# Hyena convolution with two MoE layers on one core: staged rows written in two halves, and an inverse transform in split fp32r from tile 21 on

## The chip, the cores and the metric

The kernel runs on one core of a Trainium2 chip. The metric is the device time of one launch in microseconds (us); of several runs the median is told.

## What is computed

The reference, cut to what matters:

```python
B, S, D = 2, 12480, 128
h_filt = (np.maximum(pos_emb @ w1, 0.0) @ w2) * np.exp(-0.01 * pos)[:, None]
u = x * v
Uf = np.fft.rfft(u, n=2 * S, axis=1)
Hf = np.fft.rfft(h_filt, n=2 * S, axis=0)
y = np.fft.irfft(Uf * Hf[None], n=2 * S, axis=1)[:, :S, :]
x = (x * y).reshape(B * S, D)
h = x @ moe_w_in
x = (h * np.clip(h + 3.0, 0.0, 6.0) / 6.0) @ moe_w_out
h = np.maximum(x @ moe2_w_in, 0.0)
out = h * h @ moe2_w_out
```

A long convolution along the sequence, a gate with x, and two feed-forward layers of 128 x 2048 x 128.

## The kernel before

**Convolution.** The FFT is done by matmuls. Iteration i of the main loop (some 96 of them) handles four channels and one of three signals: the filter or one of the two batches. It runs `s1` (a transform over n1, float32, 180 columns), `twiddle` (DVE, partly POOL), `split1` (ACT makes the high part h, POOL the low part l), `s2` (a transform over n2 in three fp32r matmuls of high and low parts, 360 columns), then `filt` or `prod`, `s3` (float32, back over n2) and `keep`, in which ACT gathers the result in a staging tile `stg`. Sixteen channels make a block; there are eight blocks. The loop is a software pipeline written by hand: in each round `split1` (line 202) stands ahead of `filt` or `prod`, and `keep` (line 257) at the end.

After the last `keep` of a block ACT also issues the block's rows to DRAM: `write(blk, 0)`, two small writes to `zda` (rows of tiles 0 to 3), and `write(blk, 1)`, two writes to `zdb` of 1350 KB each (the other tiles), one for each half of the 128 rows (line 360).

**Tiles.** There are 64 tiles of 390 tokens. Layer 0 of tile j and layer 1 of tile j - 20 alternate: tiles 0 to 20 of layer 0 first, then pairs (0, j), (1, j - 20), at last layer 1 alone. A tile has eight steps q. In each step PE does `l1` (six fp32r matmuls of 390 columns, line 519) and, three steps late, `l2` (six more, line 565); ACT makes `r` (relu) and `gh`, the high part of `g`; DVE makes `g` (line 535 or 538); the low part `gl` (line 548) is made by DVE in even steps and by POOL in odd ones.

Between them stands the way into layer 0. `loads` brings za, zb, the table vt and xt of a tile; `combine` (POOL, line 449) adds and subtracts za and zb to pp and pn; `s4` (line 463) is the inverse transform over k1: for each of four parts u two float32 matmuls (r = 0, 1) of 98 or 97 columns with pp or pn as weights and vt as what moves. `s4` is a generator; `between` sends one matmul at a time into PE's stream, two in a step, in steps 4 to 7 of (0, j) for tile j + 1. `gate` (line 472) multiplies the result by x, `gate_split` makes its high and low parts oh and ol (lines 478, 479), and `part1` those of layer 1, xh and xl (lines 589, 590).

The order on each engine is the order in which the program is written; nothing reorders it.

Of the kernel before, what the change touches and what calls it, by code (L numbers as in the profile page):

```python
# [7 lines left out]
F32 = mybir.dt.float32  # L8
F32R = mybir.dt.float32r
U32 = mybir.dt.uint32  # L10
AF = mybir.ActivationFunctionType
ALU = mybir.AluOpType
# [25 lines left out]

@with_exitstack
def tile_hyena_moe(ctx: ExitStack, tc, xg, vg, xT, pos, w1d, w2d, win, fmat, twc,  # L40
                   tws, dcs, inv, vtab, w_in1, w_out1, w_in2, w_out2, out):
    nc = tc.nc
    PSUM = bass.MemoryType.PSUM

# [17 lines left out]

    hs = [hp.tile([128, 32, 128], F32, tag=f"h{q}", name=f"h{q}") for q in range(4)]

    wsrc = [w_in1, w_out1, w_in2, w_out2]
    wh = {0: cp.tile([128, 2, FF], F32R, name="wp0")}

# [63 lines left out]


    def tile_loads(j, za, zb, v, x):
        nc.sync.dma_start(v, vtab[j])
        nc.sync.dma_start(x, xT[j])
        nb = NBLK - (j == 0)
        for h, t in enumerate((za, zb)):
            zr = zds[0][h, j] if j < ZA else zds[1][h, j - ZA]
            nc.sync.dma_start(t.rearrange("k d r b c -> k d (r b c)")[:, :nb],
                              zr[:nb].rearrange("d k c -> k d c"))  # L140
# [110 lines left out]
    def keep(i):  # L251
        g, s = divmod(i, 3)
        blk, ch0 = g // 4, (g % 4) * 4
        ps = ps3s.pop(i)
        if blk not in stg:
            stg[blk] = sp.tile([128, K1, 2, 2, 16], F32, name=f"stg{blk}", tag="stg")
        nc.scalar.activation(
            stg[blk][:, :, :, s - 1, ch0:ch0 + 4].rearrange("p k r c -> p r c k"),
            ps[:, :, :K4].rearrange("p r (c k) -> p r c k", c=4), AF.Copy)
        if g % 4 == 3 and s == 2:  # L260
            sv = stg.pop(blk).rearrange("p k r b c -> p k (r b c)")
            if blk == NBLK - 1:

                for h, t in enumerate((za, zb)):
                    nc.scalar.dma_start(t.rearrange("k d r b c -> k d (r b c)")[:, blk], sv[64 * h:64 * h + 1])
                tail.append(sv)
            write(blk, 0, sv)
            if blk < NBLK - 1:
                write(blk, 1, sv)


    with tc.tile_pool(name="mlp", bufs=2, side="right") as mp, \
# [83 lines left out]
    with tc.tile_pool(name="cv_ps", bufs=4, space=PSUM) as vps:  # L356
        def write(blk, z, sv, queue=nc.scalar):
            lo, hi = ((0, ZA), (ZA, 64))[z]
            for h in range(2):
                queue.dma_start(zds[z][h, :, blk], sv[64 * h + lo:64 * h + hi])  # L360

        tail = []
        s1(0)
        twiddle(0)
        s2(1)
        s1(3)
        split1(0)
        twiddle(3)
        s2(2)
        product(1, 0)  # L370
        product(1, 1)
        load(2, 0)
        load(2, 1)
        for i in range(NI + 2):

            a, z = i + AH, i - 2
            if i < NI and i not in (1, 2):
                s2(i)
            if 3 < a < NI:
                s1(a)  # L380
            if 0 <= z < NI and z % 3:
                s3(z)
            if 2 < a - 1 < NI:
                split1(a - 1)
            if 0 <= i < NI:
                if i % 3 == 0:
                    filt(i)
                else:
                    prod(i)
            if 3 < a < NI:  # L390
                twiddle(a)
            if 0 <= z < NI and z % 3:
                keep(z)
            if i == 27:
                raw_weight(1)

            for t, f in ((a + 6, load), (a + 3, product)):
                g, s = divmod(t, 3)
                if s and (2 if f is load else 1) < g < G:
                    f(g, s - 1)  # L400
            if i == NI - 1:

                room = hp.tile([128, 2, 3, FF // 4], F32, tag="h2", name="room")
                room0 = hp.tile([128, 7, 512], F32, tag="h3", name="room0")
                other = parts[(1, 3)] = decoding(None, 1, 3, nc.gpsimd)
                for _ in range(5):
                    next(other)
                decode(None, 1, 0)
                next(other)
                next(other)  # L410
                parts[(1, 1)] = decoding(None, 1, 1)
                for _ in range(5):
                    next(parts[(1, 1)])
                za, zb = (room0[:K1, k].rearrange("k (d r b c) -> k d r b c", d=NBLK, r=2, b=2) for k in (0, 1))
                vt = {0: room0[:K1, 2, :4 * N1].rearrange("k (q r n) -> k q r n", q=2, r=2)}
                xt = {0: room0[:, 3, :TOK]}
                tile_loads(0, za, zb, vt[0], xt[0])
# [7 lines left out]
    def loads(j):  # L425
        za = mo.tile([K1, NBLK, 2, 2, 16], F32, name=f"za{j}", tag="za")
        zb = mo.tile([K1, NBLK, 2, 2, 16], F32, name=f"zb{j}", tag="zb")
        vt[j] = mo.tile([K1, 2, 2, N1], F32, name=f"vt{j}", tag="vt")
        xt[j] = mo.tile([128, TOK], F32, name=f"xt{j}", tag="xt")
        tile_loads(j, za, zb, vt[j], xt[j])  # L430
        zt[j] = (za, zb)

    def combine(j):
# [13 lines left out]
        for k in range(2):  # L447
# [2 lines left out]
                                        (ALU.add, ALU.subtract)[k])  # L450
            yield

    py, ob = {}, {}

    def s4(j):

        ps = mps.tile([128, 512], F32, name=f"py{j}", tag="acc", bufs=2)
        v = vt.pop(j)
        for u in range(4):
            q, b = divmod(u, 2)  # L460
            o, n = UOFF[u]
            for r in range(2):
                nc.tensor.matmul(ps[:, o:o + n], pm[j][q][:, r, b, :],  # L463
                                 v[:, q, r, :n], start=(r == 0), stop=(r == 1))
                if u == 3 and r == 1:
                    pm.pop(j)
                    py[j] = ps
                yield

    def gate(j):  # L470
        ob[j] = mo.tile([128, TOK], F32, name=f"o{j}", tag="o")
        nc.vector.tensor_tensor(ob[j], py.pop(j)[:, :TOK], xt.pop(j), ALU.mult)

    def gate_split(j):
        o = ob.pop(j)
# [3 lines left out]
        nc.vector.tensor_tensor(l, o, h.bitcast(F32), ALU.subtract)  # L479
        xin[(0, j)] = (h, l)  # L480

    AHEAD = 20
    order = []
    for j in range(NT + AHEAD):
        if j < NT:
# [86 lines left out]
    def finish(l, j):  # L572
        ps = acc.pop((l, j))[:, :TOK]
        if l == 0:

            x1[j] = mr.tile([128, TOK], F32, name=f"x1{j}", tag="x1", bufs=AHEAD + 1)
            nc.scalar.activation(x1[j], ps, AF.Copy, scale=1.0 / 6.0)
        else:
            ot = mr.tile([128, TOK], F32, name=f"ot{j}", tag="ot")
            nc.scalar.activation(ot, ps, AF.Copy)  # L580
            nc.scalar.dma_start(out[j], ot)

# [41 lines left out]
    for n in range(len(steps) + LAG + 1):  # L624
        if n < len(steps):
            l, j, q = steps[n]
            l1(n)
        m = n - LAG
        if 0 <= m < len(steps):
            l2(m)  # L630
        if 0 <= m - 1 < len(steps) and steps[m - 1][2] == NP - 1:
            finish(*steps[m - 1][:2])
        if n < len(steps):
            if l == 0 and j < AHEAD and QS < q < QS + 3:
                (gate if q == QS + 1 else gate_split)(j + 1)
            if l == 1 and j + AHEAD + 1 < NT and q < 2:
                (gate_split if q else gate)(j + AHEAD + 1)
            if q == 6 and n + 2 < len(steps) and steps[n + 2][0] == 1:
                part1(steps[n + 2][1])
            relu(n)  # L640
            act(n)
        if 0 <= n - 1 < len(steps):
            split(n - 1)
        if n < len(steps):


            t, at = (j, (4, 7)) if l == 0 else (j + AHEAD, (1, 3))
            if t < AHEAD or l == 1:
                if q == at[0] and t + 2 < NT:
                    sums = combine(t + 2)  # L650
                if q in at and t + 2 < NT:
                    next(sums)
                if q == at[0] + 2 and t + 3 < NT:
                    loads(t + 3)

            for _ in range(2 if n < 14 else int(q not in (QS + 1, QS + 2))):
                next(rest, None)


def _tables():  # L660
# [17 lines left out]
    tt = 128 * n1[None, None, None, :] + pair[:, None, :, None]  # L678
    ph = 2 * np.pi * ((tt * (2 * k1[None, :, None, None] + 1)) % (2 * n)) / (2 * n)
    vtab = np.stack([np.cos(ph), -np.sin(ph)], axis=3) * (2.0 / n)  # L680
    pos = np.arange(S, dtype=np.float32)
    win = np.zeros(SP, np.float32)
    win[:S] = np.exp(np.float32(-0.01) * pos)
    assert not win[LF - S:].any()
    f = lambda z: np.ascontiguousarray(z, dtype=np.float32)
    return dict(win=f(np.repeat(win.reshape(N1, 2, 64).transpose(1, 2, 0).reshape(2, 64 * N1), 64, axis=0)), fmat=f(fmat), twc=f(twc), tws=f(tws),
                dcs=f(dcs), inv=f(inv), vtab=f(vtab))


def _token_index():  # L690
# [58 lines left out]
```

## Time and profile before

| | us |
|---|---|
| median of 3 runs (2830.41 to 2832.78) | 2831.36 |
| the profiled execution | 2832.95 |
| its span in the profile | 2831.1 |
| PE busy | 2765.9 (98%) |
| DVE busy | 2112.1 (75%) |
| ACT busy | 2021.9 (71%) |
| POOL busy | 1569.1 (55%) |

The span runs from the first to the last instruction; 1.85 us of the execution lie around it. PE is TensorE's matmuls, PEld its weight loads, DVE VectorE, ACT ScalarE, POOL GpSimd, SP the engine that issues most loads. A q behind an engine's name is its sequencer. PE's busy time overstates its work, since matmuls overlap and their ends are modelled. A row of a timeline gives a start, a duration, what ran how often, and in brackets the idle time before it and what ended that. Names stand as out<-in, with line numbers of the kernel before.

### The profile page before, as it was taken

How to read it: one execution, taken by the hardware profiler on the slowest of the kernel's cores; microseconds unless marked ns; L12 is line 12 of the kernel's file. 1: busy time of each engine (PE TensorE's matmuls, PEld its weight loads, DVE VectorE, ACT ScalarE, POOL GpSimd, SP SyncE). 2: the span in 40 equal slices, each digit the busy share in tenths (PEclk: the TensorE clock that was granted, in tenths of full speed). 3: DMA queues.
4: the chain of work that ended last, by engine and by line, in shares of the span. 5: the costliest groups of instructions: out<-in, count | busy, mean ns of one | idle time of the engine just before them, and what ended most of it. 6: DMA issues, size and time to landing. Idle time of an engine off the chain costs nothing.

```text
span 2831.1 us, 42236 instructions
## 1 busy us (share of the span) xinstructions
PE 2765.9 (98%) x15712; PEld 2712.0 (96%) x15712; DVE 2112.1 (75%) x2270; ACT 2021.9 (71%) x2694; POOL 1569.1 (55%) x1030
## 2 busy tenths in 40 slices
PE   7999998899999999999999999999999999999999
PEld 5888887799999999999999999999999999999999
DVE  6888888897987777777777777777777777666666
ACT  6444445687777777777777777777777777777777
POOL 3888786566665544555455545545545545444444
PEclk9999999899999999999999999999999999999999
DMA  5243433412111110001111111011111110000000
GB/s 160 92 148 105 135 110 87 108 39 71 38 35 41 27 25 23 25 25 27 27 27 27 27 27 27 24 27 27 27 27 27 27 27 17 7 12 12 12 12 15
DMA packets 139420, 125.79 MB, mean 44 GB/s; under 512 B 99692, under 2 KB 122702, under 8 KB 137806
## 3 DMA queue, kind: packets, MB, share of 16 engines
q1 hardware_dynamic: 128322, 89.23, 11.6%
q10 hardware_dynamic: 10892, 33.86, 4.0%
q8 instruction: 124, 2.03, 0.3%
q14 instruction: 82, 0.67, 0.1%
HBM read 86.64 MB, written 36.37 MB: 43 GB/s over the span
## 4 chain that ended last, share of the span: by engine, by line
PE 88%; DVE 4%; issue 3%; POOL 2%; ACT 2%; DMA 1%; ACTq 0%; POOLq 0%; SPq 0%; DVEq 0%
PE acc L565 38%; PE ph L519 38%; PE p L217 4%; PE py L463 4%; PE p L178 2%; PE p L248 1%; DVE a L194 1%; POOL l L203 1%; DVE b L188 1%; DVE p L192 1%; POOL a L241 0%; ACT h L331 0%; POOL v L155 0%; POOL a L194 0%; DVE b L236 0%
## 5 line engine op out<-in xcount | busy, mean ns | idle before, releaser
L548 POOL TENSOR_TENSOR gl<-g,gh 128x780 fp32r<-128x780 f32 x532 | 1006.1, 1891 | 1114.3 <-ACT gh L545 1109.4
L565 PE MATMUL acc<-gh,wp 128*128 128x390 f32 x4096 | 921.5, 346 | 8.0 <-DVE wp L119 8.0
L545 ACT ACTIVATE gh<-g 128x780 fp32r<-128x780 f32 x1024 | 866.6, 846 | 15.1 <-DVE g L535 13.1
L535 DVE SCALAR_TENSOR_TENSOR g<-r,ph 128x780 f32<-128x780 f32 x512 | 493.9, 965 | 338.5 <-POOL gl L548 295.0
L565 PEld LDWEIGHTS acc<-gh,wp 128*128 128x128 f32 x4096 | 730.2, 189 | 8.3 <-issue 8.3
L538 DVE SCALAR_TENSOR_TENSOR g<-ph,r 128x780 f32<-128x780 f32 x512 | 496.2, 969 | 265.1 <-POOL gl L548 240.0
L526 ACT ACTIVATE r<-ph,three 128x780 f32<-128x780 f32 x512 | 467.8, 914 | 279.5 <-PE ph L519 268.8
L519 PE MATMUL ph<-oh,wp 128*128 128x390 f32 x2048 | 633.5, 349 | 1.3 <-ACT oh L478 1.3
L519 PE MATMUL ph<-xh,wp 128*128 128x390 f32 x2048 | 616.9, 342 | 0.0
L528 ACT ACTIVATE r<-ph 128x780 f32<-128x780 f32 x512 | 422.2, 825 | 255.0 <-PE ph L519 252.6
L565 PE MATMUL acc<-gl,wp 128*128 128x390 f32 x2048 | 533.6, 341 | 3.4 <-POOL gl L548 1.7
L548 DVE TENSOR_TENSOR gl<-g,gh 128x780 fp32r<-128x780 f32 x492 | 516.1, 1049 | 0.0
L519 PEld LDWEIGHTS ph<-oh,wp 128*128 128x128 f32 x2048 | 383.8, 190 | 1.5 <-ACT oh L478 1.5
L565 PEld LDWEIGHTS acc<-gl,wp 128*128 128x128 f32 x2048 | 377.1, 189 | 5.0 <-DVE gl L548 2.6
L519 PEld LDWEIGHTS ph<-xh,wp 128*128 128x128 f32 x2048 | 380.7, 189 | 0.0
L519 PE MATMUL ph<-ol,wp 128*128 128x390 f32 x1024 | 349.4, 341 | 1.6 <-DVE ol L479 1.6
L519 PE MATMUL ph<-xl,wp 128*128 128x390 f32 x1024 | 347.6, 339 | 0.0
L202 ACT ACTIVATE h<-a 128x720 fp32r<-128x720 f32 x96 | 76.6, 804 | 221.4 <-DVE a L194 133.7
L203 POOL TENSOR_TENSOR l<-a,h 128x720 fp32r<-128x720 f32 x96 | 168.1, 1751 | 93.8 <-ACT h L202 93.8
L519 PEld LDWEIGHTS ph<-ol,wp 128*128 128x128 f32 x1024 | 193.9, 189 | 2.3 <-DVE ol L479 2.3
L519 PEld LDWEIGHTS ph<-xl,wp 128*128 128x128 f32 x1024 | 193.0, 188 | 0.0
L479 DVE TENSOR_TENSOR ol<-o,oh 128x390 fp32r<-128x390 f32 x64 | 118.4, 1850 | 10.2 <-ACT oh L478 10.2
(91 smaller groups left out, 2702.7 us busy)
## 6 DMA issues: line engine op xcount, KB each, us to landing
zdb<-stg ACTq DMA_DIRECT2D x14, 1350.0 KB
x<-xg SPq DMA_DIRECT2D x64, 196.0 KB
v<-vg SPq DMA_DIRECT2D x64, 196.0 KB
out<-ot ACTq DMA_DIRECT2D x64, 195.0 KB
xt<-xT SPq DMA_DIRECT2D x63, 195.0 KB
za<-zdb SPq DMA_DIRECT2D x60, 180.0 KB
zb<-zdb SPq DMA_DIRECT2D x60, 180.0 KB
vt<-vtab SPq DMA_DIRECT2D x63, 137.8 KB
```

The source lines that it names most:

```text
L203: nc.gpsimd.tensor_tensor(l, gt, h.bitcast(F32), ALU.subtract)
L217: nc.tensor.matmul(pv, wt, x, start=(n == 0), stop=(n == len(ops) - 1))
L463: nc.tensor.matmul(ps[:, o:o + n], pm[j][q][:, r, b, :], v[:, q, r, :n], start=(r == 0), stop=(r == 1))
L479: nc.vector.tensor_tensor(l, o, h.bitcast(F32), ALU.subtract)
L519: nc.tensor.matmul(ps[:, c, :TOK], wt, x, start=(m == 0), stop=(m == 2))
L526: nc.scalar.activation(r, ph[n][:, :, :TOK], AF.Relu, bias=three)
L528: nc.scalar.activation(r, ph[n][:, :, :TOK], AF.Relu)
L535: nc.vector.scalar_tensor_tensor(g, r, 6.0, pv, ALU.min, ALU.mult)
L538: nc.vector.scalar_tensor_tensor(g, pv, 0.0, r, ALU.max, ALU.mult)
L545: nc.scalar.activation(h, g, AF.Copy)
L548: eng.tensor_tensor(l, g, h.bitcast(F32), ALU.subtract)
L565: nc.tensor.matmul(ps, wt, x, start=(q == 0 and m == 0), stop=(q == NP - 1 and m == len(ops) - 1))
```

## The change

It has two parts. The first: `write(blk, 1)` no longer stands behind the last `keep` of a block. Its two writes go to a list, and each round of the convolution's loop that has no `keep` issues one of them on ACT.

The second: for tiles above 20, `halve` makes a high and a low part of pp and pn (ACT and DVE), POOL casts the table of the tile, which now comes from the host as a high and a low half (`vsplit`), and `s4` does three fp32r matmuls (low x high, high x low, high x high) for each float32 one, three to a yield. The output of a part is always 98 columns wide, so `gate` takes two instructions, one for each pair of parts. `halve` is called in steps 4 and 6 of (1, j), two tiles ahead, and for tile 21 in steps 0 and 1 of (0, 20). Buffers of `o` and `ot` go from two to one, those of `x1` from 21 to 20.

```diff
             write(blk, 0, sv)
             if blk < NBLK - 1:
-                write(blk, 1, sv)
+                late_rows.extend((blk, h, sv) for h in range(2))
...
             if 0 <= z < NI and z % 3:
                 keep(z)
+            elif late_rows:
+                blk, h, sv = late_rows.pop(0)
+                nc.scalar.dma_start(zds[1][h, :, blk], sv[64 * h + ZA:64 * h + 64])
...
-        nc.sync.dma_start(v, vtab[j])
+        nc.sync.dma_start(v, vtab[j] if j <= AHEAD else vsplit[j])
...
+    def halve(j, k):
+        t = pm[j][k]
+        h = mo.tile([K1, 2, 2, D], F32R, name=f"ph{j}_{k}", tag=f"pph{k}", bufs=1)
+        l = mo.tile([K1, 2, 2, D], F32R, name=f"pl{j}_{k}", tag=f"ppl{k}", bufs=1)
+        nc.scalar.activation(h, t, AF.Copy)
+        nc.vector.tensor_tensor(l, t, h.bitcast(F32), ALU.subtract)
+        if not k:
+            vr[j] = mo.tile([K1, 2, 2, 2, N1], F32R, name=f"vr{j}", tag="vr", bufs=1)
+            nc.gpsimd.tensor_copy(vr[j], vt.pop(j))
+        halves.setdefault(j, []).append((h, l))
+        if k:
+            pm[j] = halves.pop(j)
...
+        if j > AHEAD:
+            v = vr.pop(j)
+            for u in range(4):
+                q, b = divmod(u, 2)
+                hi, lo = pm[j][q]
+                ops = [(p[:, r, b, :], v[:, k, q, r, :]) for p, k in ((lo, 0), (hi, 1), (hi, 0))
+                       for r in range(2)]
+                for m, (wt, x) in enumerate(ops):
+                    nc.tensor.matmul(ps[:, N1 * u:N1 * u + N1], wt, x, start=(m == 0), stop=(m == 5))
+                    if m % 3 == 2:
+                        if u == 3 and m == 5:
+                            pm.pop(j)
+                            py[j] = ps
+                        yield
+            return
...
-        ob[j] = mo.tile([128, TOK], F32, name=f"o{j}", tag="o")
-        nc.vector.tensor_tensor(ob[j], py.pop(j)[:, :TOK], xt.pop(j), ALU.mult)
+        ob[j] = mo.tile([128, TOK], F32, name=f"o{j}", tag="o", bufs=1)
+        ps, x = py.pop(j), xt.pop(j)
+        if j <= AHEAD:
+            nc.vector.tensor_tensor(ob[j], ps[:, :TOK], x, ALU.mult)
+            return
+        for c, n in ((0, 98), (196, 97)):
+            o, xx = (t[:, c:c + 2 * n].rearrange("p (b n) -> p b n", b=2) for t in (ob[j], x))
+            pv = ps[:, c:c + 2 * N1].rearrange("p (b n) -> p b n", b=2)
+            nc.vector.tensor_tensor(o, pv[:, :, :n], xx, ALU.mult)
...
-            x1[j] = mr.tile([128, TOK], F32, name=f"x1{j}", tag="x1", bufs=AHEAD + 1)
+            x1[j] = mr.tile([128, TOK], F32, name=f"x1{j}", tag="x1", bufs=AHEAD)
...
-            ot = mr.tile([128, TOK], F32, name=f"ot{j}", tag="ot")
+            ot = mr.tile([128, TOK], F32, name=f"ot{j}", tag="ot", bufs=1)
...
                 if q == at[0] + 2 and t + 3 < NT:
                     loads(t + 3)
+                if l == 1 and q in (4, 6) and t + 2 < NT:
+                    halve(t + 2, q // 6)
+            elif j == AHEAD and q < 2:
+                halve(j + 1, q)
```

Three places in the order of instructions. The first is ACT at the end of a block of the convolution, before (stg is the staging tile, h the high part that split1 makes, hr and hq what filt makes):

```order
L257 ACTIVATE stg_819<-p_11_1181 128x2x4x90
L360 DMA zda<-stg_819 4x5760 x2
L360 DMA zdb<-stg_819 60x5760 x2
L202 ACTIVATE h_16_1226<-a_16_1193 128x720
L202 ACTIVATE h_17_1266<-a_17_1235 128x720
```

and with the change:

```order
L258 ACTIVATE stg_819<-p_11_1181 128x2x4x90
L362 DMA zda<-stg_819 4x5760 x2
L203 ACTIVATE h_16_1224<-a_16_1193 128x720
L398 DMA zdb<-stg_819 60x5760
L203 ACTIVATE h_17_1265<-a_17_1233 128x720
```

The first zdb write moves behind the next split, h_16; the second stands behind h_19, three rounds later.

The second place is PE in step 4 of a tile of layer 0, before (py is what s4 writes, ph what l1 writes, acc what l2 writes):

```order
L519 MATMUL ph_16112<-oh_15869,wp_79 128x390
L463 MATMUL py_16119<-vt_15558,pp_15881 128x98
L565 MATMUL acc_40_16094<-gh_16083,wp_4292 128x390 x4
L565 MATMUL acc_40_16094<-gl_16084,wp_4292 128x390 x2
L463 MATMUL py_16119<-vt_15558,pp_15881 128x98
L519 MATMUL ph_16136<-oh_15869,wp_79 128x390
```

and with the change:

```order
L564 MATMUL ph_11423<-oh_11170,wp_79 128x390
L490 MATMUL py_11430<-vr_11266,pl_0_11263 128x98 x2
L490 MATMUL py_11430<-vr_11266,ph_0_11262 128x98
L610 MATMUL acc_27_11405<-gh_11394,wp_4292 128x390 x4
L610 MATMUL acc_27_11405<-gl_11395,wp_4292 128x390 x2
L490 MATMUL py_11430<-vr_11266,ph_0_11262 128x98 x3
L564 MATMUL ph_11451<-oh_11170,wp_79 128x390
```

Where one float32 matmul stood, three of fp32r stand; the matmuls around them keep their places.

The third is DVE in steps 4 to 7 of a tile of layer 1, before:

```order
L538 SCALAR_TENSOR_TENSOR g_9939<-ph_9924,r_9937 128x780
L538 SCALAR_TENSOR_TENSOR g_9960<-ph_9945,r_9958 128x780
L548 TENSOR_TENSOR gl_9963<-g_9939,gh_9962 128x780
L538 SCALAR_TENSOR_TENSOR g_9981<-ph_9966,r_9979 128x780
L538 SCALAR_TENSOR_TENSOR g_10002<-ph_9987,r_10000 128x780
```

and with the change (pl is the low part of pp or pn):

```order
L583 SCALAR_TENSOR_TENSOR g_11256<-ph_11241,r_11254 128x780
L467 TENSOR_TENSOR pl_0_11263<-pp_11182,ph_0_11262 90x512
L583 SCALAR_TENSOR_TENSOR g_11283<-ph_11268,r_11281 128x780
L593 TENSOR_TENSOR gl_11286<-g_11256,gh_11285 128x780
L583 SCALAR_TENSOR_TENSOR g_11304<-ph_11289,r_11302 128x780
L467 TENSOR_TENSOR pl_1_11311<-pn_11183,ph_1_11310 90x512
L583 SCALAR_TENSOR_TENSOR g_11329<-ph_11314,r_11327 128x780
```

One subtraction stands behind the g of step 4, and one behind that of step 6.

## Rows read from the trace of the kernel before

**Rows 1.** The page: the chain that ended last, by engine.
```profile
PE 88%; DVE 4%; issue 3%; POOL 2%; ACT 2%; DMA 1%; ACTq 0%; POOLq 0%; SPq 0%; DVEq 0%
```

**Rows 2.** Windows: the stretch, its length, busy us (instructions) of each engine, clock, DMA.
```profile
core 0: us, PE busy (x) PEld busy (x) DVE busy (x) ACT busy (x) POOL busy (x), PEclk, DMA share, GB/s
75.00:490.00 415.00, 392.29 (x2112) 352.70 (x2110) 348.42 (x411) 199.17 (x259) 334.21 (x218) 0.98 0.38 114
...
905.00:2430.00 1525.00, 1525.00 (x8791) 1525.00 (x8790) 1099.25 (x1142) 1159.36 (x1520) 766.12 (x506) 1.00 0.10 26
```

**Rows 3.** Timeline of ACT and its queue around the end of a block.
```profile
176.40 0.81 ACT L202 ACTIVATE h<-a 128x720 fp32r<-128x720 f32 x1 [4.56 <-DVE a L194]
...
181.18 1.51 ACT L257 ACTIVATE stg<-p 128x720 f32<-128x720 f32 x1
182.72 0.59 ACTq L360 DMA_DIRECT2D zda<-stg  x2
183.35 5.88 ACTq L360 DMA_DIRECT2D zdb<-stg  x2
189.28 1.50 ACT L202 ACTIVATE h<-a 128x720 fp32r<-128x720 f32 x2 [6.59 <-DMA zda<-stg]
```

**Rows 4.** Timeline of PE at the same place.
```profile
190.14 0.60 PE L217 MATMUL p<-h,dcl 128*128 128x360 f32 x2 [1.29 <-DVE a L192]
191.93 0.60 PE L217 MATMUL p<-l,dch 128*128 128x360 f32 x2 [1.18 <-POOL l L203]
```

**Rows 5.** Windows of 20 us: the slice with that place, and the next.
```profile
180.00:200.00 20.00, 17.53 (x86) 15.55 (x85) 14.25 (x17) 8.89 (x11) 14.04 (x10) 0.91 0.70 206
200.00:220.00 20.00, 20.00 (x114) 18.37 (x113) 17.89 (x21) 8.99 (x14) 16.99 (x12) 1.00 0.52 159
```

**Rows 6.** The page: DMA issues of the big staged writes on ACT's queue.
```profile
zdb<-stg ACTq DMA_DIRECT2D x14, 1350.0 KB
```

**Rows 7.** Windows: the first and the last of four stretches behind a block.
```profile
138.25:141.65 3.40, 2.86 (x9) 2.86 (x10) 0.00 (x0) 1.79 (x3) 3.40 (x4) 0.50 0.97 341
...
455.70:459.10 3.40, 3.40 (x13) 3.40 (x13) 1.62 (x2) 0.34 (x2) 3.33 (x3) 0.50 0.88 307
```

**Rows 8.** Timeline of PE: starts of l2 in a plain step, then with py.
```profile
1512.15 0.88 PE L565 MATMUL acc<-gh,wp 128*128 128x390 f32 x4
...
1514.30 0.88 PE L565 MATMUL acc<-gh,wp 128*128 128x390 f32 x4
...
1516.59 0.96 PE L565 MATMUL acc<-gh,wp 128*128 128x390 f32 x4
...
1519.19 0.97 PE L565 MATMUL acc<-gh,wp 128*128 128x390 f32 x4
```

**Rows 9.** Timeline of PE's weight loads behind one transform.
```profile
1517.57 0.37 PEld L463 LDWEIGHTS py<-vt,pp 90*128 90x128 f32 x2
1517.86 0.19 PEld L519 LDWEIGHTS ph<-oh,wp 128*128 128x128 f32 x1
1517.97 0.19 PEld L519 LDWEIGHTS ph<-ol,wp 128*128 128x128 f32 x1
1518.15 0.37 PEld L519 LDWEIGHTS ph<-oh,wp 128*128 128x128 f32 x2
```

**Rows 10.** Groups: count, busy us, mean ns, idle before; 905 to 2430 us, then all.
```profile
L548 POOL TENSOR_TENSOR gl<-g,gh 128x780 fp32r<-128x780 f32 x338 | 635.5, 1880 | 759.3 <-ACT gh L545 759.3
...
L115 ACT ACTIVATE wp<-wa 128x512 fp32r<-128x512 f32 x12 | 7.5, 621 | 0.0
```

**Rows 11.** Groups of DVE from 905 to 2430 us: two subtractions of one shape.
```profile
L479 DVE TENSOR_TENSOR ol<-o,oh 128x390 fp32r<-128x390 f32 x42 | 81.3, 1936 | 7.9 <-ACT oh L478 7.9
...
L590 DVE TENSOR_TENSOR xl<-x,xh 128x390 fp32r<-128x390 f32 x43 | 24.0, 558 | 0.0
```

**Rows 12.** Timelines of DVE and of PE in a tile of layer 1.
```profile
1467.00 0.97 DVE L538 SCALAR_TENSOR_TENSOR g<-ph,r 128x780 f32<-128x780 f32 x1 [0.91 <-POOL gl L548]
1467.89 0.96 DVE L548 TENSOR_TENSOR gl<-g,gh 128x780 fp32r<-128x780 f32 x1
...
1470.30 0.52 PE L565 MATMUL acc<-gl,wp 128*128 128x390 f32 x2
```

**Rows 13.** Timeline of DVE soon after the convolution.
```profile
519.76 4.83 DVE L117 TENSOR_TENSOR room<-room,wp 128x512 f32<-128x512 f32 x1
```

More of the change, by code (lines that the diff above doesn't have):

```diff
@@ L40, in tile_hyena_moe @@
 def tile_hyena_moe(ctx: ExitStack, tc, xg, vg, xT, pos, w1d, w2d, win, fmat, twc,
-                   tws, dcs, inv, vtab, w_in1, w_out1, w_in2, w_out2, out):
+                   tws, dcs, inv, vtab, vsplit, w_in1, w_out1, w_in2, w_out2, out):
     nc = tc.nc
@@ L63, in tile_hyena_moe @@
     hs = [hp.tile([128, 32, 128], F32, tag=f"h{q}", name=f"h{q}") for q in range(4)]
+    AHEAD = 20
     wsrc = [w_in1, w_out1, w_in2, w_out2]
@@ L360, in write @@
                 queue.dma_start(zds[z][h, :, blk], sv[64 * h + lo:64 * h + hi])
-        tail = []
+        tail, late_rows = [], []
         s1(0)
@@ L427, in loads @@
         zb = mo.tile([K1, NBLK, 2, 2, 16], F32, name=f"zb{j}", tag="zb")
-        vt[j] = mo.tile([K1, 2, 2, N1], F32, name=f"vt{j}", tag="vt")
+        if j <= AHEAD:
+            vt[j] = mo.tile([K1, 2, 2, N1], F32, name=f"vt{j}", tag="vt")
+        else:
+            vt[j] = mo.tile([K1, 2, 2, 2, N1], F32, name=f"vt{j}", tag="vt")
         xt[j] = mo.tile([128, TOK], F32, name=f"xt{j}", tag="xt")
@@ L451, in combine @@
             yield
+    def halve(j, k):
[10 more added lines that the diff above has]
+            pm[j] = halves.pop(j)
+    halves, vr = {}, {}
     py, ob = {}, {}
@@ L457, in s4 @@
         ps = mps.tile([128, 512], F32, name=f"py{j}", tag="acc", bufs=2)
-        v = vt.pop(j)
+        v = vt.pop(j, None)
+        if j > AHEAD:
[13 more added lines that the diff above has]
+            return
         for u in range(4):
@@ L470, in gate @@
     def gate(j):
-        ob[j] = mo.tile([128, TOK], F32, name=f"o{j}", tag="o")
-        nc.vector.tensor_tensor(ob[j], py.pop(j)[:, :TOK], xt.pop(j), ALU.mult)
+        ob[j] = mo.tile([128, TOK], F32, name=f"o{j}", tag="o", bufs=1)
+        ps, x = py.pop(j), xt.pop(j)
+        if j <= AHEAD:
+            nc.vector.tensor_tensor(ob[j], ps[:, :TOK], x, ALU.mult)
[4 more added lines that the diff above has]
+            nc.vector.tensor_tensor(o, pv[:, :, :n], xx, ALU.mult)
     def gate_split(j):
@@ L480, in gate_split @@
         xin[(0, j)] = (h, l)
-    AHEAD = 20
     order = []
@@ L680, in _tables, with top @@
     vtab = np.stack([np.cos(ph), -np.sin(ph)], axis=3) * (2.0 / n)
+    def top(z):
+        m, e = np.frexp(z)
+        return np.ldexp(np.round(m * 4096), e - 12)
+    vt = np.stack([np.cos(ph), -np.sin(ph)], axis=3) * (2.0 / n)
+    vhi = top(vt)
     pos = np.arange(S, dtype=np.float32)
@@ L686, in _tables @@
     return dict(win=f(np.repeat(win.reshape(N1, 2, 64).transpose(1, 2, 0).reshape(2, 64 * N1), 64, axis=0)), fmat=f(fmat), twc=f(twc), tws=f(tws),
-                dcs=f(dcs), inv=f(inv), vtab=f(vtab))
+                dcs=f(dcs), inv=f(inv), vtab=f(vtab),
+                vsplit=f(np.stack([vhi, top(vt - vhi)], axis=2)))
 def _token_index():
@@ L736 @@
     names = ["xg", "vg", "xT", "pos", "w1d", "w2d", "win", "fmat", "twc", "tws", "dcs",
-             "inv", "vtab", "w_in1", "w_out1", "w_in2", "w_out2"]
+             "inv", "vtab", "vsplit", "w_in1", "w_out1", "w_in2", "w_out2"]
     aps = [nc.dram_tensor(n, arrays[n].shape, mybir.dt.from_np(arrays[n].dtype),
```

## The prediction

> **What bounds the kernel now.** I read the chain of work that ended last first: 88% of the span is PE [rows 1], so a microsecond of PE work is a microsecond of time unless PE stands still for another reason. Then the stages: in the convolution (75 to 490 us) PE is busy 392 of 415 us; from 905 to 2430 us, where tiles 21 to 63 go through the inverse transform, it is busy without a gap, at full clock, while DVE, ACT and POOL have 28%, 24% and 50% to spare [rows 2]. The change touches both stages, so each is costed by itself: in the second PE work counts in full, in the first what counts is why PE stands still. The profile's column of idle time per line comes last, for the engines beside PE.
>
> **Why PE stands still in the convolution.** After the last keep of each block of 16 channels ACT issues four staged writes in a row; the two big ones hold it for 5.88 us, and its next split waits 6.59 us for them [rows 3]. PE runs dry behind that split, twice, 1.29 and 1.18 us, 2.47 together [rows 4]; the slice from 180 to 200 us misses just that much, its neighbour none [rows 5]. Fourteen big writes stand on ACT's queue [rows 6], so seven blocks pay. After four of the seven stalls the granted clock falls from 1.00 to 0.50 (from 2.4 to 1.2 GHz) for some 3.4 us, from 138 us the first time and from 456 us the last [rows 7].
>
> **Part 1, staged rows in two halves.** The two big writes of a block leave their place behind the keep and go out one by one, in the iterations without a keep, three iterations apart, behind that iteration's split. No byte more is written, and SP's queue keeps its order. Each half holds ACT for about 2.9 us (half of 5.88). Behind the split of that iteration ACT stands idle 4.56 us now, waiting for DVE [rows 3], so the issue fits with some 1.6 us over, and the small writes that stay behind the keep (0.59 us) are no longer than the work that PE has queued. I take the stalls as gone: 7 x 2.47 = 17.3 us. With the stalls gone the clock has no cause to fall: half of PE's busy time in those stretches, 1.4 us in the first and 1.7 in the last [rows 7], some 6.5 us in four. Sum **-23.8 us**. Ends: -27 if the records hide a little of each stall behind a matmul's modelled end, -6 if each half still holds the split up for half of the stall and only the clock is won back.
>
> **Part 2, the matmuls.** A plain step of twelve 390-column matmuls takes 2.15 us from one acc to the next (1512.15 to 1514.30); a step with two float32 transforms takes 2.60 (1516.59 to 1519.19) [rows 8]. So one float32 matmul of 98 columns costs 0.225 us. It shows as two records with a weight load each (py x2), hence 0.1125 a record. Is that the columns or the loads? Twelve matmuls of 390 columns in 2.15 us are 0.46 ns a column, so 98 columns are 0.045 us; and right behind a transform the loads follow one another at 0.11 us (1517.86, 1517.97), of fp32r weights too [rows 9], where between 390-column matmuls they are 0.18 apart. A short matmul is paced by its weight load. The change makes six fp32r matmuls of two float32 ones, each with other weights than the one before, so three loads stand in place of two: 3 x 0.1125 = 0.3375 us. By tile eight such groups, 2.70 us in place of 1.80, and 43 tiles (21 to 63): 43 x 8 x 0.1125 = **+38.7 us**, on PE, which waits for nobody there. Ends from the rows: if columns alone counted, 3 x 0.045 = 0.135 us a group, -31 us; if each fp32r matmul of 98 columns were as dear as a float32 one of the same size, 0.675 a group, +155 us. I stay by the loads, since rows 9 have exactly that case, fp32r loads behind short matmuls.
>
> A rule of the Trainium skill speaks against me: FP8 and Floating Point Precision, section TensorE Precision Notes, counts a true fp32 matmul as four passes through the array. Three single passes for four would be a quarter off, 0.25 x 0.225 x 344 = -19 us, an estimate by that page. The trace's 0.225 us is five times the 0.045 of one pass of 98 columns, so passes are not what is paid here.
>
> **Part 3, the splitting.** For each tile from 21 on ACT rounds 2 x 512 elements (0.62 us each by the 512-element copy), DVE subtracts twice, POOL casts the table (784 elements; no cast by POOL is in the trace, so between nothing and the 1.88 us of its two-input subtraction of 780) [rows 10]. All three have room [rows 2] in a pair of tiles, which is 16 x 2.15 + 8 x 0.225 = 36.2 us long; what matters is the moment. The DVE subtraction reads two SBUF tiles while POOL is in its own subtraction: the like case, ol, takes 1.94 us where xl, the same shape with POOL idle, takes 0.56 [rows 11]. But there DVE waits for that same POOL result anyway, 0.91 us before the g at 1467.00 [rows 12]. So of each 1.9 us only the 0.6 us behind POOL's end is new. The gl that DVE made at 1467.89 is wanted by PE at 1470.30, 1.4 us after its end [rows 12]. A lateness of 0.6 us, and of 1.4 us with a cast of middling length in between, stays within it: **0 us**. If that cover is gone, every further microsecond in a pair is 43 us.
>
> Small edits together: the gate in two DVE instructions where there was one, the table load twice as large (the DMA share is 0.10 there [rows 2], and loads go out two tiles ahead on SP, with as many issues as before), one buffer fewer for x1, o and ot (all are read long before they are written again): 0 us, hidden by PE.
>
> **The sum.** The profiled execution took 2832.95 us: 2832.95 - 23.8 + 38.7 = 2847.9. The median of the runs is 1.6 us below it, so I forecast **2846 us**, slower by 0.5%. A measurement can tell 0.2%, 5.7 us, from no change: 2825.7 to 2837.0 is the same.
>
> **Rivals.**
> *Loads hide, columns pace (faster).* PE pulls weight loads of fp32r ahead of short matmuls and a group costs 0.135 us: 2831.4 - 23.8 - 31 = 2777 us. It turns the sign as soon as a record costs under 0.098 us, since then part 1 outweighs part 2. For it: only two loads in a row at 0.11 us are seen, never three. Against it: those two. Beside it stands the Trainium skill, TensorE: Matmul & The Clock Gate, section Back-to-back issue gap, with 81 ns for a sustained load and matmul of 128 columns; 24 x 0.081 would be 1.94 us a tile, +6 us, and 2814 us in all, an estimate by that page. No load row here comes under 0.11. The four-pass rule above belongs to this rival too: -19 in place of -31 would be 2789 us. Chance 0.10.
> *DVE and POOL in each other's way (slower).* If POOL keeps going while DVE waits, as at 519.76, where a DVE subtraction took 4.83 us [rows 13], the gl behind it comes a microsecond late and PE waits about 1 us in each pair: +43, 2889 us. It starts where DVE is over 1.4 us late. Chance 0.18.
> *Short fp32r is as dear as float32.* A group of 0.675 us: 2831.4 - 23.8 + 155 = 2963 us. For it: no fp32r matmul under 256 columns is in the trace. Chance 0.08.
> *The halves do not help.* Each half holds the split up and costs PE half a stall, and only the clock is won: 2831.4 - 6 + 38.7 = 2864 us. Against it: 4.56 us idle for 2.9. Chance 0.08.
>
> **How the numbers follow.** My forecast has 0.56; its own range is 2836 to 2856 (a record at 0.107 to 0.116 us, part 1 at -27 to -18). Taking in the rivals at 2864 and 2889 gives 2836 to 2892; left out are the faster rival, the dear matmuls and the tails, 0.20. Faster: 0.10 and a little of the low tail, 0.12. The same: 0.12, the low end of the forecast. Slower: 0.76.
>
> **What would show it.** Right: no wait of PE behind h in the convolution, clock 1.00 there; big writes of 2.9 us each behind a split; py records in threes 0.11 us apart, and a step with two groups at 2.82 us; the waits of PE from 905 us on still empty. Wrong: py records 0.05 apart (columns), or 0.2 (dear), or PE waiting for gl or py's pl in the second model's steps (rival two), or ACT's split still waiting for zdb (rival four).

## The result, and the profile after

The changed kernel takes 2854.07 us (2852.01 to 2854.79, 4 runs), the kernel before 2830.97 in the same comparison: 1.0081 times as long, 95% interval 1.0068 to 1.0094, slower by 23 us. The forecast was 2846 us, slower by 15, in a range of 2836 to 2892. The profiled execution took 2854.79 us, with a span of 2853.0 after 2831.1: 21.9 us more.

Three stretches of the trace tell where they come from. One row in each is enough: xl, the low part that opens layer 1 of a tile, by the view of its source line (count, min/median/max ns, first and last start). Before:

```profile
L590 DVE TENSOR_TENSOR xl<-x,xh x64: 556/557/561, 908.4 to 2803.1; 128x390 fp32r<-128x390 f32 x64
```

and with the change:

```profile
L635 DVE TENSOR_TENSOR xl<-x,xh x64: 555/557/562, 882.3 to 2825.0; 128x390 fp32r<-128x390 f32 x64
```

The first tile of layer 1 starts 26.1 us earlier; then the same 63 tiles take 1942.7 us in place of 1894.8, 47.9 more (these lengths are taken from starts in hundredths, as timelines give them). So part 1 gave what it should and part 2 took it back and more. This length, from the first xl to the last, comes out the same within 0.1 us in two profiles of the same kernel below, so I call it the tile stage and use it as the measure of part 2.

**The convolution.** The timeline of ACT at the end of a block answers to [rows 3]:

```profile
175.43 1.50 ACT L258 ACTIVATE stg<-p 128x720 f32<-128x720 f32 x1
176.96 0.59 ACTq L362 DMA_DIRECT2D zda<-stg  x2
177.60 0.81 ACT L203 ACTIVATE h<-a 128x720 fp32r<-128x720 f32 x1 [0.67 <-DVE a L195]
177.62 2.81 ACTq L398 DMA_DIRECT2D zdb<-stg  x1
182.82 0.81 ACT L203 ACTIVATE h<-a 128x720 fp32r<-128x720 f32 x1 [4.42 <-DVE a L195]
...
191.06 0.32 ACTq L398 DMA_DIRECT2D zdb<-stg  x1
195.07 0.81 ACT L203 ACTIVATE h<-a 128x720 fp32r<-128x720 f32 x1 [4.55 <-DVE a L195]
```

The split waits for DVE now, not for a DMA, and the big write sits inside that wait. The view of PE's waits from 75 to 480 us has no row of a block's end any more; those that stay belong to the start and the end of the convolution (columns: us in total, times, longest):

```profile
PE py L501 <- ACT pp L452: 4.9, 1, 4.9
PE ph L564 <- ACT oh L524: 1.3, 1, 1.3
PE p L218 <- DVE a L195: 1.1, 1, 1.1
...
```

and the windows say the same, against [rows 2, 5]: 2.45 of 380 us without PE, and full clock.

```profile
75.00:455.00 380.00, 377.55 (x2093) 343.81 (x2092) 342.93 (x403) 192.29 (x249) 331.12 (x215) 1.00 0.44 125
```

**The matmuls.** The timeline of PE in a tile of layer 0 answers to [rows 8]:

```profile
1508.17 0.32 PE L490 MATMUL py<-vr,pl 90*128 90x98 f32 x2
1508.33 0.28 PE L490 MATMUL py<-vr,ph 90*128 90x98 f32 x1
1508.44 0.94 PE L610 MATMUL acc<-gh,wp 128*128 128x390 f32 x4
...
1509.58 0.43 PE L490 MATMUL py<-vr,ph 90*128 90x98 f32 x3
...
1511.25 0.95 PE L610 MATMUL acc<-gh,wp 128*128 128x390 f32 x4
...
1514.07 0.95 PE L610 MATMUL acc<-gh,wp 128*128 128x390 f32 x4
```

and that of the weight loads to [rows 9]:

```profile
1509.40 0.48 PEld L490 LDWEIGHTS py<-vr,ph 90*128 90x128 f32 x3
1509.80 0.19 PEld L564 LDWEIGHTS ph<-oh,wp 128*128 128x128 f32 x1
```

From acc to acc a step with two groups (the three short matmuls that stand where one float32 matmul stood) takes 2.81 and 2.82 us, where two float32 matmuls made it 2.60: 0.11 us more a group. Four loads begin within 0.40 us of one another (1509.40 to 1509.80); the first of them still runs beside a long matmul, the rest follow at 0.11 us.

**The splitting.** The groups from 905 to 2430 us answer to [rows 10]: the operations that the trace of before lacked (the rounding of pn on ACT is like that of pp).

```profile
L467 DVE TENSOR_TENSOR pl<-pp,ph 90x512 fp32r<-90x512 f32 x41 | 68.0, 1658 | 0.0
L467 DVE TENSOR_TENSOR pl<-pn,ph 90x512 fp32r<-90x512 f32 x41 | 64.7, 1577 | 0.0
...
L470 POOL CAST vr<-vt 90x784 fp32r<-90x784 f32 x41 | 53.6, 1308 | 0.0
...
L466 ACT ACTIVATE ph<-pp 90x512 fp32r<-90x512 f32 x41 | 25.5, 622 | 0.0
L518 DVE TENSOR_TENSOR o<-py,xt 128x196 f32<-128x196 f32 x82 | 25.5, 352 | 0.0
```

DVE's subtraction takes 1.6 us beside POOL, as ol did [rows 11]; DVE goes from 1099 to 1190 us of 1525. PE does not see it: the view of PE's waits from 905 to 2470 us is empty, as before.

**What I had not forecast.** In the last stage, where layer 1 runs alone and no instruction differs, a tile takes 17.2 us where it took 17.1. The timeline of DVE, before:

```profile
2477.83 0.56 DVE L590 TENSOR_TENSOR xl<-x,xh 128x390 fp32r<-128x390 f32 x1
...
2494.94 0.56 DVE L590 TENSOR_TENSOR xl<-x,xh 128x390 fp32r<-128x390 f32 x1
...
2512.05 0.56 DVE L590 TENSOR_TENSOR xl<-x,xh 128x390 fp32r<-128x390 f32 x1
```

and with the change:

```profile
2479.78 0.56 DVE L635 TENSOR_TENSOR xl<-x,xh 128x390 fp32r<-128x390 f32 x1
...
2496.99 0.56 DVE L635 TENSOR_TENSOR xl<-x,xh 128x390 fp32r<-128x390 f32 x1
...
2514.21 0.56 DVE L635 TENSOR_TENSOR xl<-x,xh 128x390 fp32r<-128x390 f32 x1
```

That is 17.11 and 17.21 us here, 17.12 and 17.26 in the mean of twenty tiles. PE is at full clock and waits for nobody in both; each of the 96 matmuls is slower by over a nanosecond. What did change is where the tiles lie in SBUF: two larger buffers of the table less one buffer of o push gh and gl by 1568 bytes, from a start at 0 modulo 64 to one at 32. The tiles between move too (oh, ol, r and g, all by 1568 bytes), and so do xh and xl, by as much.

### The profile page after: what moved, and what is told of

The parts are those of the page before. It is cut to its first block, busy times and chain, and to the rows that moved or that the text cites. A ratio compares the mean times of both kernels' runs of the same rounds, so it can differ in the third digit from the quotient of the medians.

```text
span 2853.0 us, 43132 instructions
## 1 busy us (share of the span) xinstructions
PE 2805.8 (98%) x16056; PEld 2754.8 (97%) x16056; DVE 2238.9 (78%) x2399; ACT 2065.8 (72%) x2780; POOL 1628.0 (57%) x1073
## 4 chain that ended last, share of the span: by engine, by line
PE 94%; DVE 2%; ACT 2%; issue 1%; DMA 1%; POOL 0%; ACTq 0%; POOLq 0%; SPq 0%; DVEq 0%
PE acc L610 39%; PE ph L564 38%; PE p L218 7%; PE p L179 4%; PE py L490 3%; PE p L249 2%; PE py L501 1%; ACT h L333 1%; DVE g L580 0%; DMA zda<-stg 0%; DMA wt<-win 0%; POOL gl L593 0%; DVE a L195 0%; DMA wr<-w_in 0%; ACT stg L258 0%
```

## The experiments

Theory: the 48 us that the tile stage grew are 39 us of weight loads (three for two) and the rest is the place of gh and gl; the splitting is free; the convolution gains because ACT is not held. Rivals: columns or a switch between forms set the matmuls' price; DVE held up by POOL costs some of it; the burst of writes, not ACT's hold, starves PE; the slower plain steps come from the new work.

### The parts apart

Part 1 alone, on the kernel before:

```diff
-                write(blk, 1, sv)
+                late_rows.extend((blk, h, sv) for h in range(2))
...
+            elif late_rows:
+                blk, h, sv = late_rows.pop(0)
+                nc.scalar.dma_start(zds[1][h, :, blk], sv[64 * h + ZA:64 * h + 64])
```

> The kernel before with the staged rows in two halves and nothing else. My theory (the long issue on ACT starves PE after each block, and the clock falls behind it): the seven PE gaps of 2.5 us and the four half-clock stretches are gone, -24 to -28 us, some 2804 us. Rival (each half still holds the split up): -6, 2825 us. Rival that the gain seen in the change comes from elsewhere: 2831 us.

Measured: 2805.34 us, 0.9905 times before (0.9888 to 0.9921).

```profile
L593 DVE TENSOR_TENSOR xl<-x,xh x64: 556/559/561, 882.3 to 2777.1; 128x390 fp32r<-128x390 f32 x64
```

The tile stage starts at 882.3 us, as with the change, and is 1894.8 us long, as before. The same kernel run again later (below) gave 2804.14.

Part 2 alone, the change without those lines:

```diff
-                late_rows.extend((blk, h, sv) for h in range(2))
+                write(blk, 1, sv)
...
-            elif late_rows:
-                blk, h, sv = late_rows.pop(0)
-                nc.scalar.dma_start(zds[1][h, :, blk], sv[64 * h + ZA:64 * h + 64])
```

> The change without its first part: staged rows written as before, inverse transform in three fp32r matmuls from tile 21 on. If the parts add up: 2854 + 28 = 2882 us, seven PE gaps back, a pair of tiles at 37.16 us and a tile of the last stage at 17.26 us as in the change. If the parts depend on each other, another time.

Measured: 2880.91 us, 1.0173 (1.0158 to 1.0189); the tile stage is 1942.7 us long, the same as in the change. Against 2831.4 the parts are -26.1 and +49.5 us; their sum, +23.4, meets the change, +23.1, well within the intervals. So no dependence of the parts on each other shows.

### The place of gh and gl

A tile of 32 bytes that nobody uses, allocated ahead of gh; in the kernel before it takes gh and gl from 0 to 32 modulo 64, in the change from 32 to 0. In the kernel before nothing else moves; in the change ph, pl and vr, which lie behind gl, move by the same 32 bytes.

```diff
     def split(n):
+        if n == 0:
+            mo.tile([128, 8], F32, name="pad", tag="pad", bufs=1)
```

> The kernel before, with 32 bytes left free ahead of gh: gh and gl then begin at 32 modulo 64, as in the change, and nothing else moves. Theory that the place of gh and gl slows every plain matmul step: a tile of the last stage goes from 17.11 to 17.26 us, a pair of tiles from 36.09 to some 36.4, +13 to +17 us in all, 2846 us. Rival (the place does not matter; the slower plain steps come from the new work on the other engines or from another tile's place): 2831 us and 17.11 us a tile.

> The change, with 32 bytes left free ahead of gh: gh and gl begin at 0 modulo 64, as in the kernel before. Theory of the place: a tile of the last stage back at 17.11 us, a pair at 36.85 us, -13 to -17 us, 2838 us. Rival: 2854 us, 17.26 us a tile.

Measured: the kernel before becomes slower, 2839.66 us, 1.0028 (1.0018 to 1.0038), and the change faster, 2847.63 us, 1.0056 (1.0041 to 1.0071). The tile stage goes from 1894.8 to 1902.3 and from 1942.7 to 1936.5 us:

```profile
L637 DVE TENSOR_TENSOR xl<-x,xh x64: 555/559/562, 880.2 to 2816.7; 128x390 fp32r<-128x390 f32 x64
```

That row is of the padded change. A tile of the last stage in the padded kernel before, by the timeline of DVE:

```profile
2481.10 0.56 DVE L592 TENSOR_TENSOR xl<-x,xh 128x390 fp32r<-128x390 f32 x1
...
2498.34 0.56 DVE L592 TENSOR_TENSOR xl<-x,xh 128x390 fp32r<-128x390 f32 x1
...
2515.58 0.56 DVE L592 TENSOR_TENSOR xl<-x,xh 128x390 fp32r<-128x390 f32 x1
```

17.24 us, with the instructions of the kernel before. So the place of tiles alone slows matmuls, here by some 8 us, and 6.2 us of what the tile stage lost in the change are of this kind (of gh and gl, in the pairs perhaps with ph, pl and vr, which this run does not part). Both moved less than the 13 to 17 us that I had written down: I had multiplied the difference of the last stage by all tiles, but in the pairs it is only about 0.11 us (36.10 to 36.22 before, 37.16 to 37.06 in the change, each the mean of 42). Nor does the pad bring the last stage of the change all the way back: a tile there takes 17.17 us, not the 17.12 of before.

Is it the remainder modulo 64? The same pad, 64 bytes wide:

```diff
+            mo.tile([128, 16], F32, name="pad", tag="pad", bufs=1)
```

> The kernel before, with 64 bytes left free ahead of gh: gh and gl move, but begin at 0 modulo 64 as before. Theory that the place modulo 64 counts: no difference, 2831 us, a tile of the last stage at 17.11 us. Rival (any move of gh and gl against the other tiles costs that much): some 2839 us and 17.25 us, as with 32 bytes.

Measured: 2835.07 us, 1.0013 (1.0003 to 1.0022), tile stage 1897.9 us, between the two. So the remainder modulo 64 is not the whole of it: a move by 64 costs 3.1 us of the tile stage, one by 32 costs 7.5. Which property of the addresses counts stays open.

### What a short matmul costs

Both on the padded change. First, two products in place of three (low x high and high x high; the low half of the table is not used):

```diff
-                ops = [(p[:, r, b, :], v[:, k, q, r, :]) for p, k in ((lo, 0), (hi, 1), (hi, 0))
+                ops = [(p[:, r, b, :], v[:, k, q, r, :]) for p, k in ((lo, 0), (hi, 0))
...
```

> The change with 32 bytes ahead of gh (2847.6 us), and of the three products low x high, high x low, high x high the second left out: the low half of the table is not used, so the result lacks its part. Theory of the loads (each short matmul costs one weight load, 0.1125 us): a group costs 0.225 us as the float32 matmul did, a step with two groups takes 2.60 us, 344 x 0.1125 = -38.7 us, 2809 us. Rival (three fp32r matmuls are dear for another reason, a switch between forms at the edges of a group): less than half of that, 2830 us.

Measured: 2808.61 us, 0.9921 (0.9901 to 0.9941), 39.0 us below the padded change; tile stage 1897.0:

```profile
L637 DVE TENSOR_TENSOR xl<-x,xh x64: 555/558/561, 882.5 to 2779.5; 128x390 fp32r<-128x390 f32 x64
```

The starts of l2 by PE's timeline:

```profile
1460.30 0.94 PE L612 MATMUL acc<-gh,wp 128*128 128x390 f32 x4
...
1461.44 0.32 PE L490 MATMUL py<-vr,ph 90*128 90x98 f32 x2
...
1462.88 0.95 PE L612 MATMUL acc<-gh,wp 128*128 128x390 f32 x4
```

A step with two groups takes 2.58 us, as with float32 to within 0.02 [rows 8]. Two fp32r matmuls cost what one float32 matmul costs, and the third costs 0.11 us more. A price of the edges of a group would not have gone with the third product, so a switch between forms has no part in it.

Second, three products, but five of six matmuls over 48 columns:

```diff
-                    nc.tensor.matmul(ps[:, N1 * u:N1 * u + N1], wt, x, start=(m == 0), stop=(m == 5))
+                    c = 48 if m else N1
+                    nc.tensor.matmul(ps[:, N1 * u:N1 * u + c], wt, x[:, :c], start=(m == 0), stop=(m == 5))
```

> The change with 32 bytes ahead of gh (2847.6 us), and five of the six matmuls of each part over 48 of the 98 columns: the other columns of the inverse transform lack these products. Theory of the loads: no difference, a step with two groups at 2.82 us, 2847 us. Rival, columns pace: three records fall by 5/6 x 51%, 344 x 0.14 = -49 us, 2798 us.

Measured: 2844.27 us, 1.0049 (1.0033 to 1.0065); tile stage 1934.7 after 1936.5.

```profile
1503.36 0.27 PE L491 MATMUL py<-vr,ph 90*128 90x48 f32 x1
1503.48 0.96 PE L613 MATMUL acc<-gh,wp 128*128 128x390 f32 x4
...
1506.29 0.97 PE L613 MATMUL acc<-gh,wp 128*128 128x390 f32 x4
```

Still 2.81 us a step. Half of the columns are away in five matmuls of six and 1.8 us are won, not 49: columns do not pace these matmuls. With the first run, what is left is one price of 0.11 us for each load with its matmul. It goes with TensorE's clock: right behind the convolution of the kernel before, at a granted clock of 0.50 (1.2 GHz), eight loads of the float32 transform of tile 0 start within 1.5 us, 0.21 us apart (by the view of the tile py and a window):

```profile
L463 PEld LDWEIGHTS py<-room,pn x8: 333/333/333, 496.0 to 497.5; 90*128 90x128 f32 x8
```

```profile
496.00:497.60 1.60, 1.60 (x9) 1.60 (x9) 1.25 (x2) 0.00 (x0) 0.00 (x0) 0.50 0.38 58
```

That the price is the load's own is the plain reading of this and of [rows 9], but it is not shown: no run took the load away from a short matmul or made it smaller, so a fixed price of a matmul in the same clock stays possible. Either way matmuls are to be counted, not columns.

### The splitting without its use

The padded change does all its splitting, but the transform is float32 again, over the high half of the table alone:

```diff
-            nc.gpsimd.tensor_copy(vr[j], vt.pop(j))
+            nc.gpsimd.tensor_copy(vr[j], vt[j])
...
-        if k:
-            pm[j] = halves.pop(j)
...
         if j > AHEAD:
-            v = vr.pop(j)
...
+            v = v[:, 0]
...
-            o, n = UOFF[u]
+            o, n = UOFF[u] if j <= AHEAD else (N1 * u, N1)
```

> The change with 32 bytes ahead of gh, with all its splitting (two roundings on ACT, two subtractions on DVE, one cast on POOL for each tile), but the inverse transform is done by float32 matmuls as before, with the high half of the table alone (the low half's part is left out). Theory that the splitting costs nothing: the halves alone plus what xh and xl cost in their new place, 2805 to 2809 us, pairs at 36.1 us. Rival (DVE held up by POOL delays PE): up to a microsecond a pair, 2850 us.

Measured: 2808.43 us, 0.9920 (0.9903 to 0.9936); tile stage 1897.2, 2.5 us over before, and PE's waits from 905 to 2400 us empty:

```profile
L622 DVE TENSOR_TENSOR xl<-x,xh x64: 556/558/560, 881.3 to 2778.5; 128x390 fp32r<-128x390 f32 x64
```

All the work of ACT, DVE and POOL, the larger loads and the two-piece gate come with 2.5 us, and not all of those are theirs: in the last stage, where nothing is split, a tile takes 17.17 us after 17.12 before, 0.9 us in twenty tiles. That much is the new place of tiles, and in the pairs (36.14 after 36.10) place and work are not taken apart. The step from here to the padded change, 1897.2 to 1936.5, is the matmuls alone: 39.3 us.

### ACT's hold or the burst of writes

The two big writes stay behind the keep, back to back, but on SP's queue:

```diff
-                write(blk, 1, sv)
+                write(blk, 1, sv, nc.sync)
```

> The kernel before, with the two big staged writes of a block still issued behind its last keep and back to back, but on SP's queue. The bytes go out at the same moment as before; ACT is not held. Theory (ACT's hold is what starves PE): the PE gaps are gone, 2804 to 2808 us. Rival (the burst of writes itself is what delays something): the gaps stay, 2831 us. A third possibility: SP, held by the writes, brings the next x and v late, and new gaps stand at POOL's product.

Measured: 2862.64 us, 1.0116 (1.0099 to 1.0133): the third possibility, at a price higher than the disease. The timeline of SP's queue at the end of a block:

```profile
185.33 0.82 SPq L360 DMA_DIRECT2D zdb<-stg  x2
186.26 5.74 SPq L149 DMA_DIRECT2D x<-xg  x1
192.09 2.02 SPq L150 DMA_DIRECT2D v<-vg  x1
194.20 5.17 SPq L149 DMA_DIRECT2D x<-xg  x1
```

and PE's timeline behind it (its wait begins 19 us after the writes), with POOL's waits from 75 to 520 us:

```profile
210.62 0.97 PE L217 MATMUL p<-l,dch 128*128 128x360 f32 x2 [6.53 <-POOL l L203]
```

```profile
POOL v L155 <- DMA v<-vg: 50.9, 7, 8.0
```

The gap at the old place is gone: ACT's split is on time and PE runs through 190 us. So ACT's hold was the cause there, not the burst itself. But the hold has moved with the queue: the writes pass in 0.82 us and the loads behind them take 5.74, 2.02 and 5.17, POOL's product waits up to 8.0 us for v, seven times, and PE loses 5.6 to 6.5 us a block. Whether v is late because its issue is held or because the writes stand ahead of it in SP's queue, this run does not part.

### A version under both

Part 1 alone beats both kernels. With it I tried the other moving tiles, each beginning at 0 modulo 64 (tiles of 400 columns of which 390 are used, and a pad of 32 bytes in the pool of layer 1; the wider tiles also push gh and gl on by 128 bytes):

```diff
-        h = mo.tile([128, TOK], F32R, name=f"oh{j}", tag="oh")
+        h = mo.tile([128, 400], F32R, name=f"oh{j}", tag="oh")[:, :TOK]
...
-        h = mr.tile([128, TOK], F32R, name=f"xh{j}", tag="xh")
+        h = mr.tile([128, 400], F32R, name=f"xh{j}", tag="xh")[:, :TOK]
...
+        if j == 0:
+            mr.tile([128, 8], F32, name="pad", tag="pad", bufs=1)
```

> The kernel before with the staged rows in two halves, and with oh, ol, xh and xl all beginning at 0 modulo 64 (in the kernel before every second buffer begins at 32). If the place of any moving tile counts as that of gh and gl does: 1 to 6 us below the halves alone, 2799 to 2804 us, a tile of the last stage under 17.11 us. If only gh and gl count: 2805 us, 17.11 us.

> The kernel of the halves alone once more, beside the next one on the same chip: 2805 us, pairs at 36.09 us.

> The halves with oh, ol, xh and xl at 0 modulo 64 once more, on the same chip. If the place of those tiles counts: 2 to 4 us under the run beside it, pairs at 36.04 us. If not: no difference that can be told.

Measured: 2801.30 us, 0.9896 (0.9881 to 0.9911), the first time; side by side 2803.37, 0.9903 (0.9888 to 0.9918), against 2804.14, 0.9905 (0.9889 to 0.9922), for the halves alone. The total does not tell them apart. The tile stage does, by little: 1892.9 us twice against 1894.8 twice. The gain stands in the pairs (36.05 us after 36.10); a tile of the last stage takes 17.13 us, no less than before, against what I expected of the place. So the halves are the gain, 26 to 27 us, and the new places together add 1.9 us of the tile stage.

## Why the prediction was right

**Part 1: -23.8 forecast, -26.1 measured.** The stalls and the half-clock stretches went, within the ends of -27 and -6, and the mechanism is the one named: ACT's wait for DVE covers the issue. One reading was off: each half was to hold ACT 2.9 us, but in every block only the first does (2.64 to 2.81); the second, 12 to 13 us later, holds it 0.32. That left the cover wider than counted. Where the 2.3 us beyond the forecast come from is not shown; what a matmul's modelled end hides, the reason that the forecast gave for its end of -27, is one possibility.

**Part 2: +38.7 forecast, 39.3 measured.** The measured number is the tile stage's, which holds the transforms of 42 tiles and about half of that of tile 21; the forecast's rate gives some 38 us for them. The price of 0.1125 us a record, worked out from the steps [rows 8] and seen in two loads in a row [rows 9], held for three. That the weight load is what is paid for stays, as said, the likely reading. A step with two groups was to take 2.82 us and takes 2.81 and 2.82. The rival of the columns (2777 us) falls with the runs of two products and of 48 columns, and so does that of float32's price for fp32r (2963 us). The two rules of the Trainium skill that were weighed give other sums, and the measurement decides: by FP8 and Floating Point Precision, section TensorE Precision Notes, three single passes should have undercut the four of a true fp32 matmul, but at 98 columns two fp32r matmuls already cost as much as one float32 one; by TensorE: Matmul & The Clock Gate, section Back-to-back issue gap, a load and matmul of 128 columns go at 81 ns, and these go at 0.11 us.

**Part 3: 0 forecast, 2.5 us measured, the place of tiles included.** Part of that is the place of tiles: 0.9 us stand in the last stage, where nothing is split. DVE's subtraction took 1.6 us where I had read 1.9, POOL's cast 1.3 us, between the bounds, and PE waited for none of it. The rival of DVE and POOL (2889 us) did not come: DVE got its turn behind POOL's subtraction, as in this timeline of DVE and of POOL, and the means of 1.66 and 1.58 us over 41 tiles leave no room for subtractions of 4.83 us [rows 13] as a rule:

```profile
1493.66 1.61 DVE L467 TENSOR_TENSOR pl<-pp,ph 90x512 fp32r<-90x512 f32 x1
1495.19 0.95 DVE L583 SCALAR_TENSOR_TENSOR g<-ph,r 128x780 f32<-128x780 f32 x1
1496.07 0.95 DVE L593 TENSOR_TENSOR gl<-g,gh 128x780 fp32r<-128x780 f32 x1
```

```profile
1492.83 1.90 POOL L593 TENSOR_TENSOR gl<-g,gh 128x780 fp32r<-128x780 f32 x1 [0.99 <-ACT gh L590]
1494.65 1.31 POOL L470 CAST vr<-vt 90x784 fp32r<-90x784 f32 x1
```

pl ends 0.54 us behind POOL's subtraction (1494.73 to 1495.27), which is the 0.6 us that the forecast counted.

**What was missing.** The small edits were put at nothing, and the buffers among them are not: moving gh and gl costs 6.2 us of the tile stage, which no view of the kernel before could show as a cost. The tile stage grew by 39.3 us of matmuls, 2.5 with the splitting and 6.2 of place, 47.9 together (they are steps of one chain of kernels, so that they add up is no proof of them). With its start 26.1 us earlier that is +21.9, the difference of the profiled executions, where the forecast had +14.9; the medians differ by 23.1. The forecast's 2846 us missed by 8: this term alone is 6.2, and that no more was missed is in part luck, since the 2.5 of the splitting and the 2.3 that part 1 gained beyond its term cancel.

## What to carry to other kernels

A matmul whose columns take less than the 0.11 us of a load and matmul here costs those 0.11 us: count loads, not columns or passes. Splitting a float32 matmul of 98 columns into three fp32r ones turns two loads into three, however cheap the arithmetic looks. A long DMA issue belongs where its engine waits anyway; moved to another queue, here, it moved the hold to what stood behind it there. Before an instruction is blamed for a fraction of a per cent, compare a stage in which nothing changed: if it is slower too, look at where the tiles lie.

## What the runs showed of the hardware

- The hold of a DMA issue is not set by its size: of two equal writes of 1350 KB back to back each held ACT for about 2.9 us [rows 3]; 12 to 13 us apart, with the change, the first of a block took 2.64 to 2.81 us and the second 0.32, in all seven blocks. What sets it is not shown.
- On SP the same writes passed in 0.82 us for both, and the next load, of 196 KB, was held for 5.74 us.
- The place of the moving tiles in SBUF changes the pace of 390-column fp32r matmuls by up to 0.8% (a tile of the last stage at 17.12 or 17.25 us, kernel before and its padded version), with 32 bytes of difference and not one instruction changed; a move by 64 bytes cost less, but not nothing.
- A float32 matmul of 98 columns and two fp32r ones of the same size cost the same, 0.22 us; both are two records of a load and a matmul, 0.11 us each. At half the granted clock a record takes 0.21 us.
